# Routing of batches 1 to 7 in one run of products, with the last 64 tokens as 64 by 64 tiles

## The chip, the cores and the metric

The kernel runs on one core of a Trainium2 chip. The metric is the device time of one execution in microseconds (us), as the median of several runs. The core's engines work side by side, each from its own queue in program order: TensorE (PE for its matmuls, PEld for its weight loads), VectorE (DVE), ScalarE (ACT), GpSimd (POOL), and SyncE (SP), which issues transfers.

## The reference, cut to what matters

For 8 batches of 8 heads, 576 tokens and 64 columns, two attentions follow one another: 32 packed rows `p` per head attend to `k`, `v`, and then the tokens `q` attend to the packed result.

```
p_packed = sm_attn(p, k, v)
out      = sm_attn(q, p_packed, p_packed)
x        = out, as 8 * 576 tokens x 512 columns
xn       = x / (|x| + 1e-6);  en = expert_emb / (|expert_emb| + 1e-6)
logits   = xn @ en.T / tau
expert   = argmax(logits);  gate = the largest of softmax(logits)
y[token] = gate * relu(x @ w1[expert]) @ w2[expert]
```

The routing is the part from `xn` to `gate`: for each token the sum of squares of its 512 columns, and its 8 products with the experts' embeddings.

## The kernel before, in words

Each batch is guessed to go to one expert as a whole, whose `w1` and `w2` are loaded; a loop at the end, which runs zero times here, would repair batches for which that fails. While the feed-forward part of batch b runs (`ffn`, L953), the attention of batch b + 1 (`att_main`, L1119) is issued in small steps between its products: the loop at L1504 to L1517 calls one step per step of `ffn` (two where the attention lags behind). All order is written out by hand, and each engine takes its instructions in the order of the program.

`ffn` of a batch has 16 steps of hidden tiles (L1004, evacuated by ACT L1008 and DVE L1009), 8 steps for the last 64 tokens (L1039), and then four output tiles c = 0 to 3 of eight steps of three products each (L1057). An output tile is stored at step f = 2 of the next one (ACT L1406). In c = 3 the weights `w2` of the next batch are split at odd steps (ACT cast L909, POOL subtraction L910), and as soon as the next batch's `lg` exists, its `w1_rows` (L924) go in: products L934 into both pair-banks, then ACT L946 and DVE L947, which make `G`, the weights of the next hidden tiles. At the next batch's start `quarter_banks` (L316) takes the same pair-banks, sets parts of them by DVE (L319, L320), and `quarter_scores` (L331) writes them between the first and the second hidden tile.

PSUM has eight banks of 512 columns: three single ones in rotation ("pf", the accumulators of `ffn`), two pairs ("pb", tiles named pt), and one spare ("pu").

`route` (L757) works on `x.at` (two groups g of four heads, 128 rows by 576 tokens) and `x.ppx` (128 rows by 136 columns: packed values, then 8 columns of embedding products). A product takes 64 rows (one half) and 128 tokens, and gives 136 columns: 128 whose squares sum to the token's squared length, and 8 logits. `sums` squares the 128 columns on ACT with a running sum (L778, an ACTIVATE and a READ_ACCUMULATOR) and adds the 8 columns up on DVE (L781). For batches 1 to 7 it runs in these turns, each at one step of the loop (`TURNS`, L1080, r a step of `route`, f a flip of the next batch's keys, DVE L291):

```
TURNS = "r", "r", "r", "f", "f", "ff", "r", "r", "r", "r", "r"
```

The first turn issues the products of token tiles 0 and 1 into the two pair-banks, turns 1 and 2 their sums; turns 3 to 5 flip keys; turn 6 issues tiles 2, 3 and 4 into the same pair-banks (tile 4, the last 64 tokens, as tiles of 128 whose first half is not used), and turns 7 to 10 their sums and the rest: two adds (L819, L820), the scaling and the argmax (L822 to L834), and a memset on POOL (L838), after which `x.lg` exists. Turn 0 falls on c = 2, f = 0, turn 6 on c = 2, f = 6, and turn 10 on c = 3, f = 2 (for batch 1 one step earlier). Batch 7 has no next batch; its token counts (`counts`, L846) follow three steps later.

Of the kernel before, what the change touches and what calls it, by code (L numbers as in the profile page):

```python
# [9 lines left out]
F32 = mybir.dt.float32  # L10
# [3 lines left out]
AF = mybir.ActivationFunctionType  # L14
ALU = mybir.AluOpType
AX = mybir.AxisListType

P = 128
HB = 4
NC5 = 5  # L20
# [7 lines left out]
def kernel(  # L28
# [12 lines left out]
    nc = tc.nc  # L41
    B, H, S, D = q.shape
    E, DM, F = w1.shape
    NP = p.shape[2]
    NG = H // HB
# [4 lines left out]
    XW = 2 * D + E  # L50
# [6 lines left out]
    sm = ctx.enter_context(tc.tile_pool(name="sm", bufs=2))  # L57
    ps = ctx.enter_context(tc.tile_pool(name="ps", bufs=3, space=bass.MemoryType.PSUM))
    pb = ctx.enter_context(tc.tile_pool(name="pb", bufs=2, space=bass.MemoryType.PSUM))

    pc = ctx.enter_context(tc.tile_pool(name="pc", bufs=1, space=bass.MemoryType.PSUM))
# [11 lines left out]
    for h in range(HB):  # L73
        nc.vector.memset(pairs[32 * h : 32 * h + 32, h // 2 : h // 2 + 1], 1.0)
        for g in range(NG):
            at = (h ^ g) % 2
# [163 lines left out]
    def rows(c):  # L240
        return P if c < 4 else 64
# [513 lines left out]


    def route(x):  # L757
        lg = sm.tile([P, NC5, E], F32, name="lg", tag="lg")
        ss = sm.tile([P, NC5], F32, name="ss", tag="ss")
        nc.gpsimd.memset(lg[:64, 4:5, :], 0.0)  # L760
        nc.gpsimd.memset(ss[:64, 4:5], 1.0)
        def product(c, g, to):
            n = min(c * P, S - P)
            for half in range(2):
                at = slice(64 * half, 64 * half + 64)
                nc.tensor.matmul(  # L766
                    to[:, half],
                    x.at[at, g, n : n + P],
                    x.ppx[at, g],
                    start=True,  # L770
                    stop=True,
                    tile_position=(64 * half, 0),
                )

        def sums(c, pt, lgs, sss):
            r = slice(P - rows(c), P)
            scr = sb.tile([P, 2, NG, 2 * D], F32, name="scr", tag="scr")
            nc.scalar.activation(  # L778
                scr[r, :, : pt.shape[2]], pt[r, :, :, : 2 * D], AF.Square, accum_out=sss[r]
            )  # L780
            nc.vector.tensor_reduce(  # L781
                lgs[r],
                pt[r, :, :, 2 * D :].rearrange("p h g w -> p w h g"),
                axis=AX.XY,
                op=ALU.add,
            )

        def units():
            pt = pb.tile([P, 1024], F32, name="pt", tag="pb")
            return pt.rearrange("p (h w) -> p h w", h=2)[:, :, : 3 * XW].rearrange(  # L790
                "p h (u w) -> p h u w", u=3
            )

        if x is bat[0]:
            for c in range(NC5):
                pt = units()
                for g in range(NG):
                    product(c, g, pt[:, :, g])
                yield
                sums(c, pt[:, :, :NG], lg[:, c], ss[:, c : c + 1])  # L800
        else:
            lg4 = sm.tile([P, E], F32, name="lg4", tag="lg4", bufs=1)
            ss4 = sm.tile([P, 1], F32, name="ss4", tag="ss4", bufs=1)
            for cs in ((0, 1), (2, 3)):
                pts = [units() for _ in cs]
                for c, pt in zip(cs, pts):
                    for g in range(NG):
                        product(c, g, pt[:, :, g])
                if cs[0]:
                    for g, pt in enumerate(pts):  # L810
                        product(4, g, pt[:, :, NG])
                yield
                for c, pt in zip(cs, pts):
                    sums(c, pt[:, :, :NG], lg[:, c], ss[:, c : c + 1])
                    yield
            sums(4, pts[0][:, :, NG:], lg[:, 4], ss[:, 4:5])
            sums(4, pts[1][:, :, NG:], lg4, ss4)
            yield
            nc.vector.tensor_tensor(out=lg[64:, 4], in0=lg[64:, 4], in1=lg4[64:], op=ALU.add)  # L819
            nc.vector.tensor_tensor(out=ss[64:, 4:5], in0=ss[64:, 4:5], in1=ss4[64:], op=ALU.add)  # L820

        nc.vector.tensor_scalar_mul(lg, lg, itau)  # L822
        mx = sm.tile([P, NC5, 1], F32, name="lmx", tag="lmx")
        nc.vector.tensor_reduce(mx, lg, axis=AX.X, op=ALU.max)
        nc.vector.tensor_tensor(
            out=lg, in0=lg, in1=mx.broadcast_to([P, NC5, E]), op=ALU.subtract
        )
        oh = sm.tile([P, NC5, E], F32, name="oh", tag="oh")
        nc.vector.scalar_tensor_tensor(
            out=oh, in0=lg, scalar=0.0, in1=code.broadcast_to([P, NC5, E]),  # L830
            op0=ALU.is_ge, op1=ALU.mult,
        )
        nc.vector.tensor_reduce(mx, oh, axis=AX.X, op=ALU.max)
        nc.vector.tensor_tensor(  # L834
            out=oh, in0=code.broadcast_to([P, NC5, E]), in1=mx.broadcast_to([P, NC5, E]),
            op=ALU.is_equal,
        )
        nc.gpsimd.memset(oh[:64, 4], 0.0)  # L838
        x.oh = oh
        x.lg, x.ss = lg, ss  # L840
# [236 lines left out]
            drain(after.w1g)  # L1077

    AHEAD = 3
    TURNS = "r", "r", "r", "f", "f", "ff", "r", "r", "r", "r", "r"  # L1080
    STF = 2

    def out_rows(b, c):
# [35 lines left out]
    def att_main(b):  # L1119
# [27 lines left out]
        if b:  # L1147
            steps = {"r": route(x), "f": flips}
            if b == 1:
                next(flips)  # L1150
            for turn in TURNS:
                for step in turn:
                    next(steps[step], None)
                yield
# [295 lines left out]
    def route_first():  # L1450
        yield from route(bat[0])
        yield from idle(2)
        counts(bat[0])

    with tc.manual_schedule():
# [65 lines left out]
        out=rest_f, in0=rest_f, scalar1=-1.0, scalar2=float(S), op0=ALU.mult, op1=ALU.add  # L1521
# [6 lines left out]
    with tc.If(n_rest > 0):  # L1528
        with tc.For_i(0, B, 1) as b:
            nb = nc.values_load(rest_i[0:1, ds(b, 1)], min_val=0, max_val=S)  # L1530
            with tc.If(nb > 0):
                x = Batch()
# [3 lines left out]
                drain(att1(x, nat))  # L1536
                drain(att2(x))
                drain(route(x))
                counts(x)
                drain(gates(x))  # L1540
# [5 lines left out]
                    out=ge, in0=x.oh, in1=x.gate.unsqueeze(2).broadcast_to([P, NC5, E]),  # L1546
                    op=ALU.mult,
# [70 lines left out]
```

## Time and profile before

| | us |
|---|---|
| median of 3 runs | 420.41 |
| lowest and highest | 420.27, 420.61 |
| the profiled execution's own time | 420.91 |
| its span, first to last instruction | 419.2 |
| mean granted TensorE clock, share of full speed | 0.995 |

The profile shows one execution. Its own time is the span and what lies around it. Times in the rows below are in us from the span's start, and L12 is line 12 of the kernel. A row of a timeline merges neighbouring instructions of the same kind: start, length, engine, line, operation, what it writes and reads, shapes, count, and in brackets the idle time of the engine before it and what ended it ("issue": nothing that the profile shows).

### The profile page before, as it was taken

The numbers are of one execution on the slowest core, as the hardware profiler recorded it, in microseconds if no ns is written. First come the engines' busy times: TensorE is split into PE (matmuls) and PEld (weight loads), VectorE is DVE, ScalarE is ACT, GpSimd is POOL, SyncE is SP. The second block draws the span as 40 slices with busy tenths as digits, with TensorE's granted clock in tenths as the row PEclk, the third lists the DMA queues.
The fourth block names the chain that finished last, engine by engine and source line by source line (L and its number), as shares of the span: only waits on it lengthen the run. The fifth ranks groups of instructions, "written<-read, shape, count | busy, mean of one in ns | idle before, by whom it ended". The sixth has DMA issues, their size and how long they took to land.

```text
span 419.2 us, 11033 instructions
## 1 busy us (share of the span) xinstructions
PE 408.4 (97%) x4036; PEld 327.9 (78%) x4037; DVE 307.2 (73%) x941; ACT 202.5 (48%) x473; POOL 158.7 (38%) x197
## 2 busy tenths in 40 slices
PE   7899999999999999999999999999999999999993
PEld 4758677697878978698777978789786987779783
DVE  3677696588977889769886889778897798566500
ACT  4577705762365714754146622656146631576110
POOL 2345714437204561336414381136613273142200
PEclk9999999999999999999999999999999999999998
DMA  8999896977999479886999669886899819310012
GB/s 225 331 338 236 220 296 221 229 189 187 298 298 235 116 216 294 284 201 172 267 316 228 169 172 280 301 216 177 225 317 262 195 39 344 121 48 5 20 48 54
DMA packets 42607, 87.93 MB, mean 210 GB/s; under 512 B 11690, under 2 KB 20906, under 8 KB 42546
## 3 DMA queue, kind: packets, MB, share of 16 engines
q1 hardware_dynamic: 35280, 61.44, 54.2%
q0 software_dynamic: 6720, 25.17, 18.4%
q8 instruction: 34, 0.56, 0.6%
q10 hardware_dynamic: 546, 0.54, 0.6%
q14 instruction: 27, 0.22, 0.2%
HBM read 77.68 MB, written 9.44 MB: 208 GB/s over the span
## 4 chain that ended last, share of the span: by engine, by line
PE 91%; DMA 4%; ACT 1%; DVE 1%; POOL 1%; SPq 0%; issue 0%; ACTq 0%; POOLq 0%
PE pf L1057 43%; PE pf L1004 24%; PE pf L1039 7%; PE pt L766 5%; DMA nat<-in_k 4%; PE pt L934 3%; PE pt L396 2%; PE pt L270 2%; PE pt L331 2%; PE pt L1233 1%; PE pu L501 0%; DMA out<-o 0%; PE pt L477 0%; PE pu L512 0%; ACT st L689 0%; PE pt L464 0%
## 5 line engine op out<-in xcount | busy, mean ns | idle before, releaser
L1057 PE MATMUL pf<-w2s,hT 128*128 128x512 f32 (+1 forms) x792 | 183.9, 388 | 0.0
L1057 PEld LDWEIGHTS pf<-w2s,hT 128*128 128x128 f32 x792 | 143.1, 188 | 39.3 <-issue 9.4
L910 POOL TENSOR_TENSOR w2s<-w2r,w2s 128x512 fp32r<-128x512 f32 x64 | 81.2, 1285 | 86.1 <-ACT w2s L909 85.3
L1004 PE MATMUL pf<-AT,G 128*128 128x288 f32 x720 | 102.1, 298 | 0.4 <-DVE hT L1009 0.2
L1004 PEld LDWEIGHTS pf<-AT,G 128*128 128x128 f32 x720 | 97.2, 188 | 4.3 <-issue 1.5
L1009 DVE SCALAR_TENSOR_TENSOR hT<-pf,hT 128x224 fp32r<-128x224 f32 (+1 forms) x128 | 52.2, 413 | 30.3 <-ACT hT L1008 29.9
L1008 ACT ACTIVATE hT<-pf 128x224 fp32r<-128x224 f32 (+1 forms) x128 | 49.3, 386 | 42.8 <-PE pf L1004 40.1
L1406 ACT ACTIVATE o<-pf,gate 128x512 f32<-128x512 f32 (+1 forms) x41 | 26.0, 635 | 32.2 <-PE pf L1057 21.2
L909 ACT CAST w2s<-w2r 128x512 fp32r<-128x512 f32 x64 | 38.7, 618 | 0.2
L291 DVE STREAM_TRANSPOSE kt<-nat 128x576 f32<-128x576 f32 x52 | 38.1, 759 | 0.0
L778 ACT ACTIVATE scr<-pt 128x512 f32<-128x512 f32 (+2 forms) x47 | 25.0, 532 | 18.0 <-PE pt L766 17.0
L1039 PE MATMUL pf<-w2r,h 128*64 128x256 f32 x256 | 33.3, 388 | 0.0
L715 POOL TENSOR_TENSOR AT<-at,AT 128x576 fp32r<-128x576 f32 x7 | 9.9, 1411 | 49.1 <-ACT AT L710 49.1
L383 POOL TENSOR_TENSOR qs<-p 128x320 f32<-128x320 f32 x12 | 10.6, 881 | 45.4 <-ACT p L364 45.4
L689 ACT ACTIVATE st<-st 128x576 f32<-128x576 f32 (+1 forms) x17 | 11.1, 657 | 33.8 <-DVE st L686 32.6
L872 ACT ACTIVATE lg<-lg 128x40 f32<-128x40 f32 x8 | 1.9, 237 | 48.4 <-DVE lg L868 48.4
L781 DVE TENSOR_REDUCE lg<-pt 128x8 f32<-128x32 f32 (+2 forms) x47 | 8.7, 185 | 22.0 <-ACT scr L778 21.7
L766 PEld LDWEIGHTS pt<-ppx,at 64*128 64x128 f32 x320 | 19.7, 186 | 6.2 <-issue 3.6
L1039 PEld LDWEIGHTS pf<-w2r,h 128*64 128x64 f32 x256 | 19.4, 137 | 4.9 <-PE pu L501 1.0
L766 PE MATMUL pt<-ppx,at 64*128 64x136 f32 x320 | 23.1, 287 | 0.0
L710 ACT CAST AT<-at 128x576 fp32r<-128x576 f32 x15 | 10.1, 675 | 22.6 <-DVE at L704 22.5
L364 ACT ACTIVATE p<-pt,qnm 128x160 f32<-128x160 f32 x48 | 17.8, 398 | 0.0
(213 smaller groups left out, 474.9 us busy)
## 6 DMA issues: line engine op xcount, KB each, us to landing
nat<-in_q SPq DMA_DIRECT2D x112, 140.0 KB, 3.5
nat<-in_k SPq DMA_DIRECT2D x96, 140.0 KB, 4.0
w1t<-in_moe_w POOLq DMA_DIRECT2D x12, 1024.0 KB, 9.3
w2r<-in_moe_w POOLq DMA_DIRECT2D x24, 512.0 KB, 16.0
out<-o SPq DMA_DIRECT2D x124, 64.0 KB, 2.1
w2r<-in_moe_w SPq DMA_DIRECT2D x8, 512.0 KB, 10.3
vn<-in_v SPq DMA_DIRECT2D x24, 160.0 KB, 3.8
vn<-in_v SPq DMA_DIRECT2D x48, 80.0 KB, 3.9
```

The costliest lines, as they stand in the source:

```text
L291: nc.vector.transpose(kt.rearrange("p (c i) -> p c i", i=32), t)
L364: nc.scalar.activation(x.p1[g][:, n * QW : n * QW + QW], area(x, g)[:, n // 2, n % 2], AF.Exp, bias=x.nm[:, at : at + 1],)
L766: nc.tensor.matmul(to[:, half], x.at[at, g, n : n + P], x.ppx[at, g], start=True, stop=True, tile_position=(64 * half, 0),)
L778: nc.scalar.activation(scr[r, :, : pt.shape[2]], pt[r, :, :, : 2 * D], AF.Square, accum_out=sss[r])
L909: nc.scalar.copy(t[:, 0], raw)
L910: nc.gpsimd.tensor_tensor(out=t[:, 1], in0=raw, in1=t[:, 0].bitcast(F32), op=ALU.subtract)
L1004: nc.tensor.matmul(pf[:, :HS], w, r, start=(n == 0), stop=(n == len(ops) - 1))
L1008: nc.scalar.activation(hT[:, 0, f, cs], pf[:, :n], AF.Relu)
L1009: nc.vector.scalar_tensor_tensor(out=hT[:, 1, f, cs], in0=pf[:, :n], scalar=0.0, in1=hT[:, 0, f, cs].bitcast(F32), op0=ALU.max, op1=ALU.su ...
L1039: nc.tensor.matmul(pf[64 * hf : 64 * hf + 64, :256], h4[:, f], x.w2r[f // 2][:, f % 2, hf * 256 : hf * 256 + 256], start=(f == 0), stop=(f ...
L1057: nc.tensor.matmul(pf[:, :w], hT[:, a, f, c * P : (c + 1) * P], x.w2s[f][:, m, at : at + w], start=(f == 0 and i == 0), stop=(f == NF - 1 ...
L1406: nc.scalar.activation(o[:, :w], pf[:, :w], AF.Copy, scale=x.gate[:, c : c + 1])
```

## The change

Batches 1 to 7 now issue all routing products in one turn. Token tiles 0 and 1 go to the first two places of the two pair-banks, tile 2 to their third places, tile 3 to the spare bank and one accumulator bank (one row half each), and the last 64 tokens to the third places of these two, as products of 64 rows by 64 token columns at four places of the array (row half by g). `lg` and `ss` become parts of one tile, so that one add can join both. Sums are taken in eight parts, and four small DVE steps join them. The key flips come before the products. Batch 0 keeps its way.

```diff
     def route(x):
-        lg = sm.tile([P, NC5, E], F32, name="lg", tag="lg")
-        ss = sm.tile([P, NC5], F32, name="ss", tag="ss")
+        both = sm.tile([P, NC5, E + 1], F32, name="lg", tag="lg")
+        lg, ss = both[:, :, :E], both[:, :, E]
...
+        def product(at, g, half, to, tokens, column=0):
+            nc.tensor.matmul(
+                to,
+                x.at[at, g, tokens],
+                x.ppx[at, g],
+                start=True,
+                stop=True,
+                tile_position=(64 * half, column),
+            )
...
-            lg4 = sm.tile([P, E], F32, name="lg4", tag="lg4", bufs=1)
-            ss4 = sm.tile([P, 1], F32, name="ss4", tag="ss4", bufs=1)
-            for cs in ((0, 1), (2, 3)):
-                pts = [units() for _ in cs]
-                for c, pt in zip(cs, pts):
-                    for g in range(NG):
-                        product(c, g, pt[:, :, g])
-                if cs[0]:
-                    for g, pt in enumerate(pts):
-                        product(4, g, pt[:, :, NG])
-                yield
-                for c, pt in zip(cs, pts):
-                    sums(c, pt[:, :, :NG], lg[:, c], ss[:, c : c + 1])
-                    yield
-            sums(4, pts[0][:, :, NG:], lg[:, 4], ss[:, 4:5])
-            sums(4, pts[1][:, :, NG:], lg4, ss4)
-            yield
-            nc.vector.tensor_tensor(out=lg[64:, 4], in0=lg[64:, 4], in1=lg4[64:], op=ALU.add)
-            nc.vector.tensor_tensor(out=ss[64:, 4:5], in0=ss[64:, 4:5], in1=ss4[64:], op=ALU.add)
+            pts = [units() for _ in range(2)]
+            ones_of = [
+                pool.tile([P, 512], F32, name=name, tag=name)[:, : 3 * XW].rearrange(
+                    "p (u w) -> p u w", u=3
+                )
+                for pool, name in ((pc, "pu"), (ps, "pf"))
+            ]
+            banks = [[pts[0][:, h], pts[1][:, h], ones_of[h]] for h in range(2)]
+            for c, spots in enumerate((
+                ((0, 0), (0, 1)), ((1, 0), (1, 1)), ((0, 2), (1, 2)), ((2, 0), (2, 1)),
+            )):
+                for g, (n, u) in enumerate(spots):
+                    for half, at in enumerate(halves):
+                        product(at, g, half, banks[half][n][:, u], slice(c * P, c * P + P))
+            for g in range(NG):
+                for half, at in enumerate(halves):
+                    product(
+                        at, g, half, ones_of[half][halves[g], 2], slice(4 * P, S), 64 * g
+                    )
+            yield
+            part = sm.tile([P, 6, E + 1], F32, name="part", tag="pbd", bufs=1)
+            lgx, ssx, every = part[:, :, :E], part[:, :, E], slice(0, P)
+            for n in range(2):
+                sums(every, pts[n][:, :, :NG], lg[:, n], ss[:, n : n + 1])
+                sums(every, pts[n][:, :, NG:], lgx[:, n], ssx[:, n : n + 1])
+                yield
+            for lo, us in ((2, slice(0, NG)), (4, slice(NG, 3))):
+                for n, t in enumerate(ones_of):
+                    sums(every, t[:, us].unsqueeze(1), lgx[:, lo + n], ssx[:, lo + n : lo + n + 1])
+                yield
+            pair = part.rearrange("p (c n) e -> p c n e", n=2)
+            nc.vector.tensor_tensor(
+                out=both[:, 2:4], in0=pair[:, :2, 0], in1=pair[:, :2, 1], op=ALU.add
+            )
+            one, two = part[:, 4], part[:, 5]
+            nc.vector.tensor_tensor(out=one, in0=one, in1=two, op=ALU.add)
+            nc.vector.tensor_copy(two[rest], one[:64])
+            nc.vector.tensor_tensor(out=both[rest, 4], in0=one[rest], in1=two[rest], op=ALU.add)
...
-    TURNS = "r", "r", "r", "f", "f", "ff", "r", "r", "r", "r", "r"
+    TURNS = "", "", "", "f", "ff", "f", "r", "r", "r", "r", "rr"
```

The products thus fall in turn 6, the sums in turns 7 to 10, and `x.lg` exists after turn 10 as before.

## Rows read from the trace of the kernel before

**Rows 1.** The page: busy time of each engine; the chain that ended last.
```profile
PE 408.4 (97%) x4036; PEld 327.9 (78%) x4037; DVE 307.2 (73%) x941; ACT 202.5 (48%) x473; POOL 158.7 (38%) x197
...
PE 91%; DMA 4%; ACT 1%; DVE 1%; POOL 1%; SPq 0%; issue 0%; ACTq 0%; POOLq 0%
```

**Rows 2.** Timeline of TensorE's weight loads, batch 2's routing inside batch 1's outputs.
```profile
113.54 0.87 PEld L1057 LDWEIGHTS pf<-w2s,hT 128*128 128x128 f32 x4
114.76 1.00 PEld L766 LDWEIGHTS pt<-ppx,at 64*128 64x128 f32 x16 [0.35 <-issue]
115.88 3.99 PEld L1057 LDWEIGHTS pf<-w2s,hT 128*128 128x128 f32 x18
120.23 1.46 PEld L766 LDWEIGHTS pt<-ppx,at 64*128 64x128 f32 x24 [0.35 <-DVE kt L291]
121.82 2.59 PEld L1057 LDWEIGHTS pf<-w2s,hT 128*128 128x128 f32 x12
...
129.95 0.95 PEld L1004 LDWEIGHTS pf<-AT,G 128*128 128x128 f32 x6
131.06 0.94 PEld L331 LDWEIGHTS pt<-kt,pw 64*32 64x32 f32 x64 [0.16 <-issue]
```

**Rows 3.** Timeline of ScalarE, the same stretch.
```profile
121.77 0.60 ACT L778 ACTIVATE scr<-pt 128x512 f32<-128x512 f32 x1 [2.30 <-PE pt L766]
...
122.49 0.60 ACT L778 ACTIVATE scr<-pt 128x512 f32<-128x512 f32 x1
...
123.21 0.38 ACT L778 ACTIVATE scr<-pt 64x256 f32<-64x256 f32 x1
...
123.83 0.38 ACT L778 ACTIVATE scr<-pt 64x256 f32<-64x256 f32 x1
...
124.33 0.62 ACT L909 CAST w2s<-w2r 128x512 fp32r<-128x512 f32 x1
```

**Rows 4.** Timeline of VectorE, the same stretch.
```profile
118.29 0.18 DVE L781 TENSOR_REDUCE lg<-pt 128x8 f32<-128x32 f32 x1
...
119.10 2.76 DVE L291 STREAM_TRANSPOSE kt<-nat 128x576 f32<-128x576 f32 x4
...
124.34 0.18 DVE L781 TENSOR_REDUCE lg<-pt 64x8 f32<-64x16 f32 x1 [0.33 <-ACT scr L778]
...
125.33 1.03 DVE L825 TENSOR_TENSOR lg<-lg,lmx 128x40 f32<-128x40 f32 x1
...
126.86 0.20 DVE L834 TENSOR_TENSOR oh<-code,lmx 128x40 f32<-128x40 f32 x1
127.11 2.36 DVE L947 TENSOR_TENSOR G<-pt,G 128x1024 fp32r<-128x1024 f32 x2
...
129.75 0.11 DVE L320 MEMSET pt<- 64x64 f32 x1
```

**Rows 5.** Timeline of GpSimd, the same stretch.
```profile
125.03 1.28 POOL L910 TENSOR_TENSOR w2s<-w2r,w2s 128x512 fp32r<-128x512 f32 x1 [9.51 <-ACT w2s L909]
127.12 0.10 POOL L838 MEMSET oh<- 64x8 f32 x1 [0.82 <-DVE oh L834]
```

**Rows 6.** Timeline of all engines, batch 1's routing.
```profile
75.46 0.24 DVE L822 TENSOR_SCALAR lg<-lg,itau 128x40 f32<-128x40 f32 x1
...
75.97 0.20 DVE L825 TENSOR_TENSOR lg<-lg,lmx 128x40 f32<-128x40 f32 x1
...
76.67 0.20 DVE L834 TENSOR_TENSOR oh<-code,lmx 128x40 f32<-128x40 f32 x1
...
80.59 0.11 DVE L320 MEMSET pt<- 64x64 f32 x1
...
82.39 0.94 PEld L331 LDWEIGHTS pt<-kt,pw 64*32 64x32 f32 x64 [0.16 <-issue]
```

**Rows 7.** Timeline of TensorE's weight loads, batch 7's routing.
```profile
363.68 1.46 PEld L766 LDWEIGHTS pt<-ppx,at 64*128 64x128 f32 x24 [0.35 <-issue]
...
372.36 0.09 PEld L846 LDWEIGHTS pu<-oh,ones 128*1 128x1 f32 x2 [0.35 <-issue]
```

More of the change, by code (lines that the diff above doesn't have):

```diff
@@ L757, in route, with sums @@
     def route(x):
-        lg = sm.tile([P, NC5, E], F32, name="lg", tag="lg")
-        ss = sm.tile([P, NC5], F32, name="ss", tag="ss")
+        both = sm.tile([P, NC5, E + 1], F32, name="lg", tag="lg")
+        lg, ss = both[:, :, :E], both[:, :, E]
         nc.gpsimd.memset(lg[:64, 4:5, :], 0.0)
         nc.gpsimd.memset(ss[:64, 4:5], 1.0)
[L762 to L776, printed above, removed]
+        def product(at, g, half, to, tokens, column=0):
[7 more added lines that the diff above has]
+            )
+        def sums(r, pt, lgs, sss):
             scr = sb.tile([P, 2, NG, 2 * D], F32, name="scr", tag="scr")
+            to = scr.rearrange("p h g w -> p (h g w)")[r, : pt.shape[1] * pt.shape[2] * 2 * D]
             nc.scalar.activation(
-                scr[r, :, : pt.shape[2]], pt[r, :, :, : 2 * D], AF.Square, accum_out=sss[r]
+                to.rearrange("p (h g w) -> p h g w", h=pt.shape[1], g=pt.shape[2]),
+                pt[r, :, :, : 2 * D], AF.Square, accum_out=sss[r],
             )
@@ L792, in units @@
             )
+        rest = slice(64, P)
+        halves = [slice(64 * half, 64 * half + 64) for half in range(2)]
         if x is bat[0]:
@@ L796, in route @@
                 pt = units()
+                n = min(c * P, S - P)
                 for g in range(NG):
-                    product(c, g, pt[:, :, g])
+                    for half, at in enumerate(halves):
+                        product(at, g, half, pt[:, half, g], slice(n, n + P))
                 yield
-                sums(c, pt[:, :, :NG], lg[:, c], ss[:, c : c + 1])
+                sums(slice(P - rows(c), P), pt[:, :, :NG], lg[:, c], ss[:, c : c + 1])
         else:
-            lg4 = sm.tile([P, E], F32, name="lg4", tag="lg4", bufs=1)
@@ L803, in route @@
-            ss4 = sm.tile([P, 1], F32, name="ss4", tag="ss4", bufs=1)
-            for cs in ((0, 1), (2, 3)):
-                pts = [units() for _ in cs]
-                for c, pt in zip(cs, pts):
-                    for g in range(NG):
-                        product(c, g, pt[:, :, g])
-                if cs[0]:
-                    for g, pt in enumerate(pts):
-                        product(4, g, pt[:, :, NG])
-                yield
-                for c, pt in zip(cs, pts):
-                    sums(c, pt[:, :, :NG], lg[:, c], ss[:, c : c + 1])
-                    yield
@@ new lines, in route @@
+            banks = [[pts[0][:, h], pts[1][:, h], ones_of[h]] for h in range(2)]
[6 more added lines that the diff above has]
+            for g in range(NG):
+                for half, at in enumerate(halves):
+                    product(
+                        at, g, half, ones_of[half][halves[g], 2], slice(4 * P, S), 64 * g
+                    )
```

## The prediction

> **What bounds the kernel now.** I read the page first: its engine line and the chain of waits [rows 1]. TensorE is busy 97% of the span and the chain that ended last is 91% TensorE, so time is won or lost only where TensorE's own queue gets shorter or has to wait. [...] The routing products (L766) stand in two groups between the output products (L1057). From the last output load's end to the next output load's start the first group costs 115.88 - (113.54 + 0.87) = 1.47 us with 16 records, the second 121.82 - (115.88 + 3.99) = 1.95 us with 24. The eight records more are two pairs (two row halves side by side, two passes each), so a pair is 0.24 us, and each group has a fixed 1.47 - 4 x 0.24 = 0.51 us, of which 0.35 us is the idle time ahead of it. No stall lies in there: the 0.35 us put down to L291 in the second group is as long as that of the first group, which waits for nothing. So two groups cost 3.42 us a batch, 1.02 us of it for going in and out twice.
>
> Last I followed who must be ready behind the routing: ScalarE's Squares [rows 3], VectorE [rows 4] and GpSimd [rows 5]. Squares, reduces, the argmax steps (L822 to L834), G's low part (L947) and the bank memsets (L319, L320) make one chain that ends in the scores of the next batch (L331, 131.06). The needed memset is done at 129.75 + 0.11 = 129.86, so the chain has 1.2 us of slack and TensorE waits for none of it. The batches repeat: batches 2 to 6 have the same offsets.
>
> **The change, part by part.** *TensorE.* One group instead of two: one fixed 0.51 us goes. Sixteen of the products (eight pairs) stay as they are, 1.92 us. The last 64 tokens were two pairs, 0.48 us; as four tiles of 64 by 64 they go side by side, for which I take one pair's 0.24 us (0.48 would mean that nothing is gained). New is a change of tile shape inside the group, from 64*128 to 64*64. No row shows that one. It can cost nothing, or as much as the idle time on the way in, 0.35; I take the way out, 0.51 - 0.35 = 0.16, because it also follows a short product. New group: 0.51 + 1.92 + 0.24 + 0.16 = 2.83 us, 0.59 less a batch (0.40 to 0.75 by the ends).
> The Trainium skill (TensorEngine Tiling (Array Packing), Key Properties) says that changing the tiling mode, though not the tile, drains the engine, which speaks against the inner change. By that rule it costs as an entry does and the gain is 0.40; the rows cannot tell, having no such change behind short products but the way out.
>
> *Banks.* Besides the two pair-banks the group now takes the spare bank and one of the three accumulator banks. The next use of that accumulator is the second hidden tile of the next batch, some 12 us later, and the spare bank's is later still: cost nothing, covered by c = 3's 24 output products; without that cover a hidden tile would wait for the last Squares.
>
> *ScalarE.* Let T be the first routing load of the new group. It comes when the second group did, less the first group's 1.47: T = 120.23 - 1.47 + 0.04 (the gap between loads that stays) = 118.80. The six Squares, two of which used to be done by then, become eight, all behind T. The first Square of the second group started 1.54 after that group's first load [rows 2, 3], behind the fifth pair, which is the last to write its tile; the new group also has five pairs up to there, so 1.54 stands. A 512-column Square lasts 0.72 until the next, a 256-column one 0.50 to 0.62 (123.83 to 124.33, 123.21 to 123.83); I take 0.50, and by the same slope 0.39 for 128 columns. A reduce never starts before the Square on its banks has ended [rows 3, 4], so I take the reverse too: the Squares on the third unit of a pair-bank wait for the reduce ahead of them, 0.27 us each, twice (lower end: no wait). The Trainium skill (PSUM — Partial Sum Buffer, on bank collisions) has two engines kept apart on a bank for reads as well. That gives T + 1.54, 2.52, 3.02, 3.97, 4.47, 4.97; then the w2 cast (L909, issued after turn 9, so now between the Squares) from 5.47 with 0.62; the last two Squares at 6.09 and 6.48; the last reduce at 6.90. In the old order the last reduce came at 124.34 - 120.23 = 4.11 behind its group.
>
> *VectorE.* The four key flips (2.76 us) move ahead of all reduces. They can start at 118.29, where the first group's first reduce stands now, and end at 121.05, just when the first reduce wants to start (T + 2.26): no cost. The sums now take four small steps in place of two. The first is a two-input add from SBUF, as L825 is: that one takes 1.03 us while GpSimd's L910 runs and ends 0.05 behind it [rows 4, 5], but 0.20 in batch 1, where no L910 runs beside it [rows 6]. GpSimd's L910 starts 0.70 behind the start of the cast: 5.47 + 0.70 + 1.28 = 7.45, so the add ends at 7.50 (without the lock 7.3). Copy and second add at 0.24 each (five steps take 1.21 in [rows 6]): L822 at 7.98. From there to the end of L834 it is 1.41 unlocked [rows 6]: L825 now gains 0.83, because the next L910 stands behind the memset L838 in GpSimd's queue, and that waits for L834. L834 ends at 9.40, L947 starts at 9.45, the first pair of memsets ends 2.75 later as it does now [rows 4], and L331 can start 0.05 after: T + 12.25, that is 131.05.
>
> *What waits for it.* TensorE without a stall would come to the hidden tile at 129.95 - 0.59 = 129.36 and to L331 1.11 later. The first half of G is ready at T + 9.45 + 1.18 (half of the 2.36 in [rows 4]) = 129.43, a wait of 0.07; then L331, at 130.54, waits for the memsets until 131.05. Before, it started at 131.06. So in batches 2 to 6 the stall takes back the 0.59: gain 0.0.
>
> *Batches 1 and 7.* In batch 1 the memset is done at 80.70 and L331 starts at 82.39, a slack of 1.7 [rows 6]; the cast stands behind all Squares there and no L910 runs beside the adds, so the chain shifts by less and 0.59 stays. In batch 7 there are no memsets, but the count (L846, at 372.36 [rows 7]) wants L838, which comes at T + 9.6 with T = 363.68 - 1.43 = 362.25, so 371.9 with its end, against 371.77: 0.45 stays.
>
> *Other queues.* The flips' freed buffers let SP issue the query loads under a microsecond earlier; the kernel waits for no load there, cost nothing. GpSimd's two memsets of the sums move from turn 0 to turn 6, into idle time.
>
> **Sum.** 0.59 + 5 x 0.0 + 0.45 = 1.0 us less. The profiled execution took 420.91 (span 419.2 and 1.7 around it), so it would take 419.9; the median of the runs is 0.5 lower, 420.41, and so is the forecast: 419.4.
>
> **Rivals.**
> *The gain stays everywhere.* If the Squares on the third units need not wait for the reduces, the chain is 0.54 shorter, L331 could start at 130.51 and TensorE would be there at 130.47. For it: no row shows a Square behind a reduce. Against: the reduces wait for the Squares every time. Gain 6 x 0.59 + 0.45 = 4.0, time 416.4. With the drain of the Trainium skill (TensorEngine Tiling (Array Packing), Key Properties) it would be 6 x 0.40 + 0.26 = 2.7, time 417.7.
> *The chain is longer and the kernel slower.* Place: L331's wait for the memsets in batches 2 to 6. If the four 256-column Squares take 0.62 instead of 0.50, L331 comes 0.48 later than now, 5 x 0.48 - 1.0 = 1.4 us slower, 421.8. For it: one of the two Squares of that size does take 0.62. Against: the other doesn't. It decides from a delay of 0.38 a batch on; a further wait of the same size anywhere between the first Square and L947 does the same.
> *The quad gains nothing.* The four tiles run as two pairs: batches 1 and 7 lose 0.24 each, the others are set by the chain all the same; 0.5 us less in all, 419.9, no change that could be told.
>
> **How the numbers follow.** About 0.2%, 0.84 us, is what a measurement of this kernel can tell from no change. The forecast (stall takes back the gain, L331 within 0.3 us of its old place) has 0.57: -1.0 - 5 x 0.3 to -1.0 + 5 x 0.3, 417.9 to 420.9; it falls in two, about 0.31 faster and 0.26 within 0.2%. The whole gain has 0.18, the longer chain 0.20, the quad without gain 0.05. Faster 0.31 + 0.18 = 0.49, same 0.26 + 0.05 = 0.31, slower 0.20. The range, 417.0 to 421.9, leaves out the lower half of the whole gain and what lies above a delay of 0.5.
>
> **What would show it.** In the changed profile L766 stands once per batch with 0.35 idle ahead of it and 40 records in about 2.3 us from first load to last. The second Square starts behind the first reduce, not directly behind the first Square. L825 takes 0.2 in all batches, and L331 has idle time of about 0.6 us ahead of it, ended by VectorE's memsets, in batches 2 to 6 but not in batch 1. It is wrong if L331 waits for nothing (the gain is then 3 us or more), if idle time shows up at L1057 or L1004 outside these places, or if a hidden tile waits for an accumulator bank.

## The result and the profile after

The changed kernel takes 423.27 us, the median of 14 runs, against 420.99 for the kernel before in as many: 1.0054 of it, 95% interval 1.0039 to 1.0069. It is slower by 2.3 us, where 1.0 us less was forecast and the range ended at 421.9. Both kernels scatter by some 2.5 us from execution to execution, part of it in the first 35 us, ahead of any routing; what follows therefore compares stretches inside the profiles.

The page of the changed kernel: the engines' busy time, and the chain that ended last, by engine and by line.

```profile
PE 407.5 (96%) x4036; PEld 326.6 (77%) x4037; DVE 308.3 (73%) x969; ACT 202.9 (48%) x501; POOL 158.6 (38%) x197
...
PE 67%; DVE 12%; DMA 9%; ACT 6%; issue 3%; SPq 1%; POOL 1%; ACTq 0%; DVEq 0%; POOLq 0%
PE pf L1080 26%; PE pf L1027 23%; PE pf L1062 6%; DMA nat<-in_k 6%; ACT scr L776 4%; DVE G L970 3%; DMA out<-o 3%; PE pt L764 2%; PE pt L396 2%; PE pt L331 2%; PE pt L270 1%; PE pt L957 1%; DVE kt L291 1%; DVE lg L837 1%; SPq L194 1%
```

TensorE is busy 0.9 us less than in [rows 1], yet its share of the chain fell from 91% to 67%: followed back from its end, the chain now leaves TensorE for the routing's Squares (L776) and VectorE's steps. That share says which path was followed, not how long TensorE stands still: of the kernels below, "early store" has 68% and is faster than the kernel before, and "order alone" has 91% with a gap of 2.42 us. Where TensorE waits, and for how long, the weight loads tell. Here are those of batch 1's routing in the changed kernel (L764 is the routing product, L1080 the output product, L957 `w1_rows`).

```profile
70.08 1.46 PEld L764 LDWEIGHTS pt<-ppx,at 64*128 64x128 f32 x24 [0.35 <-DVE pw L299]
72.53 1.23 PEld L1080 LDWEIGHTS pf<-w2s,hT 128*128 128x128 f32 x6 [0.18 <-issue]
76.62 1.23 PEld L1080 LDWEIGHTS pf<-w2s,hT 128*128 128x128 f32 x6 [2.87 <-issue]
78.27 0.23 PEld L957 LDWEIGHTS pt<-w1t,T 64*32 64x32 f32 x16 [0.42 <-issue]
79.13 0.22 PEld L957 LDWEIGHTS pt<-w1t,T 64*32 64x32 f32 x8 [0.63 <-issue]
79.98 0.22 PEld L957 LDWEIGHTS pt<-w1t,T 64*32 64x32 f32 x8 [0.64 <-issue]
81.70 3.97 PEld L1080 LDWEIGHTS pf<-w2s,hT 128*128 128x128 f32 x18 [1.51 <-issue]
...
86.83 0.94 PEld L331 LDWEIGHTS pt<-kt,pw 64*32 64x32 f32 x64 [0.16 <-issue]
```

Six output products behind the routing, that is two steps, TensorE stands still for 2.87 us. These are the last two steps of c = 2; what waits is the first product of c = 3. Batches 2 to 7 have no such gap: their longest idle time between weight loads is 0.84 us, as in the kernel before. The chain of waits names what ended it (start, length, what):

```profile
76.11 0.20 ACT scr L776
76.31 0.02 issue
76.34 0.17 DVE part L780
76.51 0.09 DVE lg L837
76.60 0.05 issue
76.65 1.69 PE pf L1080 x6
```

The routing's last Square, its last reduce on the accumulator bank (L780, done at 76.51), then the output tile. L837, the first add, stands in between only because it runs on the same engine: TensorE's queue begins to take its next work at 76.55, just behind the reduce and before L837 ends at 76.59. ScalarE's stores (L1429) on both sides of the gap show why that bank was needed: c = 0 is stored ahead of the routing's Squares, c = 1 only in c = 3, behind the gap.

```profile
69.88 0.68 ACT L1429 ACTIVATE o<-pf,gate 128x512 f32<-128x512 f32 x1
...
78.16 0.68 ACT L1429 ACTIVATE o<-pf,gate 128x512 f32<-128x512 f32 x1
```

The loads behind the gap are also slower: the 32 records of L957 and what lies around them take 81.70 - 78.27 = 3.43 us. The windows view shows why (PE, PEld, DVE, ACT and POOL busy, granted clock, DMA share, GB/s):

```profile
76.62:78.27 1.65, 1.62 (x6) 1.05 (x6) 1.34 (x8) 0.64 (x2) 0.00 (x0) 0.94 0.91 240
78.27:81.70 3.43, 3.43 (x33) 0.66 (x32) 0.65 (x3) 1.94 (x3) 1.37 (x2) 0.53 1.11 242
81.70:85.70 4.00, 4.00 (x25) 3.30 (x18) 2.58 (x6) 2.86 (x5) 3.42 (x3) 1.00 1.07 239
```

In the stretch that begins 1.65 us behind the gap the granted clock is 0.53, nearly all of it at 1.2 GHz instead of 2.4, and is back at 1.00 in the stretch from 81.70.

Batch 2 went much as predicted, some 4.4 us later in the span. Its weight loads, where [rows 2] show the kernel before:

```profile
123.30 1.46 PEld L764 LDWEIGHTS pt<-ppx,at 64*128 64x128 f32 x24 [0.35 <-issue]
...
125.75 2.61 PEld L1080 LDWEIGHTS pf<-w2s,hT 128*128 128x128 f32 x12 [0.18 <-issue]
...
133.90 0.95 PEld L1027 LDWEIGHTS pf<-AT,G 128*128 128x128 f32 x6
135.40 0.96 PEld L331 LDWEIGHTS pt<-kt,pw 64*32 64x32 f32 x64 [0.55 <-PE pf L1027]
```

Its Squares, in place of [rows 3]:

```profile
124.84 0.60 ACT L776 ACTIVATE scr<-pt 128x512 f32<-128x512 f32 x1 [2.20 <-PE pt L764]
...
125.78 0.39 ACT L776 ACTIVATE scr<-pt 128x256 f32<-128x256 f32 x1 [0.26 <-DVE lg L780]
...
126.29 0.60 ACT L776 ACTIVATE scr<-pt 128x512 f32<-128x512 f32 x1
...
127.24 0.39 ACT L776 ACTIVATE scr<-pt 128x256 f32<-128x256 f32 x1 [0.26 <-DVE lg L780]
...
128.63 0.61 ACT L932 CAST w2s<-w2r 128x512 fp32r<-128x512 f32 x1
```

And VectorE, in place of [rows 4]:

```profile
125.56 0.19 DVE L780 TENSOR_REDUCE lg<-pt 128x8 f32<-128x32 f32 x1
...
129.94 0.17 DVE L780 TENSOR_REDUCE part<-pf 128x8 f32<-128x8 f32 x1 [0.23 <-ACT scr L776]
130.02 0.61 DVE L837 TENSOR_TENSOR lg<-part 128x18 f32<-128x18 f32 x1
...
131.73 0.20 DVE L848 TENSOR_TENSOR lg<-lg,lmx 128x40 f32<-128x40 f32 x1
...
132.54 2.35 DVE L970 TENSOR_TENSOR G<-pt,G 128x1024 fp32r<-128x1024 f32 x2
...
135.17 0.11 DVE L320 MEMSET pt<- 64x64 f32 x1
```

The second and fourth Squares wait 0.26 us each for a reduce; the first add (L837) takes 0.61 and ends 0.03 behind GpSimd's subtraction (L933, from 129.32 to 130.60); the argmax subtraction (L848, 1.03 us in [rows 4]) takes 0.20; and L331 has 0.55 us of idle time ahead of it, 0.16 before. The view of that line names what ended the idle time in batches 2 to 6 (sum in us, times), first that ahead of its weight loads, then that ahead of its products:

```profile
  PE pf L1027: 2.7, 5
  DVE pt L320: 1.7, 5
```

The products wait for the memset L320, and so does the first load, though its row names the hidden tile: it starts at 135.40, behind the memset's end at 135.17 + 0.11 = 135.28, while the hidden tile's last load ends at 133.90 + 0.95 = 134.85. The memset thus holds TensorE five times.

All profiles of this study, cut into the same stretches by the weight loads (us; "first hidden tile" is the start of the first one in batch 0 with `G` as weights, "batch 1" is from there to L331 of batch 2, "batches 2 to 6" from there to L331 of batch 7, "batch 7" from there to its first hidden tile; "time" is the median of all runs, and the ratio to the kernel before and its 95% interval come from the same sets of runs, though the ratio is not the quotient of the two medians):

| kernel | first hidden tile | batch 1 | batches 2 to 6 | batch 7 | time | ratio | interval |
|---|---|---|---|---|---|---|---|
| before | 34.63 | 47.76 | 243.44 | 47.96 | 420.99 | | |
| changed | 35.15 | 51.68 | 242.89 | 47.48 | 423.27 | 1.0054 | 1.0039 to 1.0069 |
| changed, again | 35.21 | 49.99 | 242.93 | 47.48 | 423.11 | 1.0040 | 1.0022 to 1.0057 |
| early store | 34.54 | 47.30 | 242.88 | 47.45 | 419.22 | 0.9952 | 0.9933 to 0.9972 |
| batch 1 old | 34.55 | 47.84 | 242.94 | 47.45 | 419.80 | 0.9969 | 0.9953 to 0.9985 |
| early store and order | 34.26 | 47.22 | 240.94 | 47.46 | 417.74 | 0.9922 | 0.9903 to 0.9942 |
| order alone | 36.26 | 49.61 | 240.97 | 47.46 | 420.97 | 0.9986 | 0.9972 to 1.0000 |
| before, early store | 34.78 | 47.85 | 243.61 | 47.99 | 421.20 | 1.0004 | 0.9990 to 1.0017 |

The changed kernel loses 3.9 us in batch 1, gains 0.11 in each of the next five, and 0.5 in batch 7. The start differs by up to 2.0 us between profiles, before any routing.

### The profile page after: what moved, and what is told of

Same layout as the page of the kernel before. It is cut to its first block, busy times and chain, and to the rows that moved or that the text cites. A ratio compares the mean times of both kernels' runs of the same rounds, so it can differ in the third digit from the quotient of the medians.

```text
span 423.0 us, 11100 instructions
## 1 busy us (share of the span) xinstructions
PE 407.5 (96%) x4036; PEld 326.6 (77%) x4037; DVE 308.3 (73%) x969; ACT 202.9 (48%) x501; POOL 158.6 (38%) x197
## 4 chain that ended last, share of the span: by engine, by line
PE 67%; DVE 12%; DMA 9%; ACT 6%; issue 3%; SPq 1%; POOL 1%; ACTq 0%; DVEq 0%; POOLq 0%
PE pf L1080 26%; PE pf L1027 23%; PE pf L1062 6%; DMA nat<-in_k 6%; ACT scr L776 4%; DVE G L970 3%; DMA out<-o 3%; PE pt L764 2%; PE pt L396 2%; PE pt L331 2%; PE pt L270 1%; PE pt L957 1%; DVE kt L291 1%; DVE lg L837 1%; SPq L194 1%
## 5 line engine op out<-in xcount | busy, mean ns | idle before, releaser
L1080 PE MATMUL pf<-w2s,hT 128*128 128x512 f32 (+1 forms) x792 | 182.1, 387 | 2.5 <-DVE lg L837 2.5
L1080 PEld LDWEIGHTS pf<-w2s,hT 128*128 128x128 f32 x792 | 143.6, 188 | 42.5 <-issue 14.3
L933 POOL TENSOR_TENSOR w2s<-w2r,w2s 128x512 fp32r<-128x512 f32 x64 | 80.9, 1283 | 85.0 <-ACT w2s L932 82.7
L1429 ACT ACTIVATE o<-pf,gate 128x512 f32<-128x512 f32 (+1 forms) x41 | 26.0, 634 | 27.3 <-PE pf L1080 16.4
L776 ACT ACTIVATE scr<-pt 128x512 f32<-128x512 f32 (+2 forms) x33 | 16.8, 508 | 20.3 <-PE pt L764 16.4
L970 DVE TENSOR_TENSOR G<-pt,G 128x1024 fp32r<-128x1024 f32 x14 | 16.5, 1217 | 3.1 <-ACT G L969 3.1
L922 POOL DMA_DIRECT2D w2r<-in_moe_w x24 | 17.0, 713 | 0.0
L764 PEld LDWEIGHTS pt<-ppx,at 64*128 64x128 f32 x208 | 12.7, 187 | 3.7 <-issue 2.5
```

The source lines that it names most:

```text
L764: nc.tensor.matmul(to, x.at[at, g, tokens], x.ppx[at, g], start=True, stop=True, tile_position=(64 * half, column),)
L776: nc.scalar.activation(to.rearrange("p (h g w) -> p h g w", h=pt.shape[1], g=pt.shape[2]), pt[r, :, :, : 2 * D], AF.Square, accum_out=sss[r],)
L933: nc.gpsimd.tensor_tensor(out=t[:, 1], in0=raw, in1=t[:, 0].bitcast(F32), op=ALU.subtract)
L970: nc.vector.tensor_tensor(out=to[1], in0=src, in1=to[0].bitcast(F32), op=ALU.subtract)
L1080: nc.tensor.matmul(pf[:, :w], hT[:, a, f, c * P : (c + 1) * P], x.w2s[f][:, m, at : at + w], start=(f == 0 and i == 0), stop=(f == NF - 1 ...
L1429: nc.scalar.activation(o[:, :w], pf[:, :w], AF.Copy, scale=x.gate[:, c : c + 1])
```

## The experiments

The theory: the output tile c = 3 of batch 0 waits for the accumulator bank that the routing has borrowed, because the tiles of c = 1 and c = 2 still hold the other two. The rivals put the loss on an accident of one execution, on every batch instead of batch 1, or on the longer chain by itself; the expectations give each its numbers. The kernel before was run again beside them: 421.22 us beside the first four, 420.98 beside the last two.

**The changed kernel again**, unaltered.

> The changed kernel once more, unaltered. Both theories expect the same +2.3 us against the kernel before (0.5%). What it tells: whether batch 1's idle time of 2.9 us ahead of the last output tile of batch 0 (c = 3) and the low granted clock behind it (0.53 of full speed from 78.3 to 81.7 us in the first profile) come again. Theory A (accumulator bank): the idle time comes again at the same place, within 0.3 us, since it hangs on the order of the program alone. Theory B (a late transfer or another disturbance of that one execution): it moves or goes.

Measured: 1.0040, interval 1.0022 to 1.0057. The gap came again, to the hundredth, but the low clock did not; the weight loads, then the windows view:

```profile
76.59 1.23 PEld L1080 LDWEIGHTS pf<-w2s,hT 128*128 128x128 f32 x6 [2.87 <-issue]
78.18 0.18 PEld L957 LDWEIGHTS pt<-w1t,T 64*32 64x32 f32 x16 [0.36 <-issue]
```

```profile
76.59:78.18 1.59, 1.56 (x7) 1.05 (x7) 1.28 (x8) 0.59 (x2) 0.00 (x0) 1.00 0.98 239
78.18:80.05 1.87, 1.87 (x33) 0.48 (x32) 0.38 (x2) 1.29 (x3) 1.38 (x2) 1.00 1.09 223
```

L957's stretch takes 1.87 us here and 3.43 in the first profile. So the gap belongs to the program's order and is no accident of one execution (theory B falls), and the clock is a second price, which the first profile paid and this one did not. Of the 24 executions of the two sets, 12 have a mean granted clock of 0.992 or less, and their median is 423.8; the other 12 have 0.994 or more, and 422.4. Among 26 executions of the three kernels below without the gap there is none under 0.995, and of 48 of the kernel before, run beside these and the later experiments, two are at 0.992. A mean does not tell where the clock was low, though: the profile of "order alone" below has 0.993, with 0.84 and 0.82 from 5 to 15 us, ahead of any routing, and 1.00 behind its gap. That the gap brings the lower clock is thus suggested, and not shown.

**Early store.** `ffn` of batch 0 keeps its output tiles one longer (`late`); the edit lets c = 1 be stored in c = 2, and with it c = 2 in c = 3 instead of at the end.

```diff
-                    if f == STF and len(last) > late:
+                    while f == STF and len(last) > (late and c < 2):
                         store(*last.pop(0))
```

> One edit: the feed-forward part of batch 0 stores its output tile c = 1 two steps into c = 2, together with c = 0, instead of two steps into c = 3. Theory A: batch 0 stores one tile late, so at the start of c = 3 the accumulators of c = 1 and c = 2 are still held and the only bank left is the one that the routing took; c = 3 waits for the routing's last Square and reduce. With c = 1 stored early its bank is free: no idle time ahead of c = 3, no low clock, batch 1 gains 0.5 us instead of losing 3.9. Whole kernel 1.6 us less than the kernel before (0.5 in batch 1, 0.12 in each of batches 2 to 6, 0.5 in batch 7). Theory B (the long chain of Squares, reduces and adds itself holds TensorE, whatever bank c = 3 takes): the idle time stays at 2.5 us or more and the time stays 2.3 us above the kernel before.

Measured: 0.9952 (0.9933 to 0.9972), about 2.0 us less than the kernel before. ScalarE's two stores ahead of the Squares, then the weight loads of batch 1:

```profile
69.26 1.26 ACT L1429 ACTIVATE o<-pf,gate 128x512 f32<-128x512 f32 x2
```

```profile
69.45 1.46 PEld L764 LDWEIGHTS pt<-ppx,at 64*128 64x128 f32 x24 [0.35 <-DVE pw L299]
71.90 2.61 PEld L1080 LDWEIGHTS pf<-w2s,hT 128*128 128x128 f32 x12 [0.18 <-issue]
74.87 0.18 PEld L957 LDWEIGHTS pt<-w1t,T 64*32 64x32 f32 x16 [0.35 <-issue]
```

All twelve output loads run through and the gap is gone, while the Squares, the reduces and TensorE's order are unchanged. The store of c = 2 cannot have done it, since it comes only within c = 3. So it was the bank, not the chain by itself. Batch 1 takes 47.30 us, 0.46 less than before; the other stretches stay as in the changed kernel.

**Batch 1 the old way**: the old branch of `route` and the old turns for batch 1 alone.

```diff
+        elif x is bat[1]:
+            for cs in ((0, 1), (2, 3)):
...
-            for turn in TURNS:
+            for turn in FIRST if b == 1 else TURNS:
...
+    FIRST = "r", "r", "r", "f", "f", "ff", "r", "r", "r", "r", "r"
```

> Batch 1 alone is routed the old way (two groups of products, old turns); batches 2 to 7 stay as changed. Theory A: the whole loss sits in batch 1, so the time is 1.1 us less than that of the kernel before (5 x 0.12 + 0.5), with no stretch of low clock. Rival C (the loss is spread: the accumulator or the longer chain costs in every batch): the time stays above the kernel before, by 1 us or more.

Measured: 0.9969 (0.9953 to 0.9985), 1.3 us less. Batch 1 is back at 47.84 us (47.76 before), the rest as changed: the whole loss sat in batch 1, and rival C falls.

**Early store and another order of the Squares.**

```diff
             for n in range(2):
                 sums(every, pts[n][:, :, :NG], lg[:, n], ss[:, n : n + 1])
-                sums(every, pts[n][:, :, NG:], lgx[:, n], ssx[:, n : n + 1])
-                yield
+            yield
+            for n in range(2):
+                sums(every, pts[n][:, :, NG:], lgx[:, n], ssx[:, n : n + 1])
+            yield
```

> The early store of the run before, and the Squares in another order: first the two of 512 columns on the two pair-banks, then the two of 256 columns on their third places, so that none follows the reduce of its own banks directly. Theory A (the prediction's chain: in batches 2 to 6 the scores of the next batch wait for the memsets, and two Squares wait 0.26 us each for a reduce): the chain is 0.5 us shorter, the idle time of 0.55 us ahead of the next batch's scores shrinks to the 0.16 us of the kernel before, and each of batches 2 to 6 gains 0.4 to 0.5 us: 3.6 to 4.1 us less than the kernel before. Rival D (that idle time comes from something else than this chain): the same 1.6 us less as with the early store alone, and the 0.55 us stay.

Measured: 0.9922 (0.9903 to 0.9942), 3.3 us less by the ratio and 3.5 by the medians, a little short of the 3.6 to 4.1 expected. ScalarE, then the weight loads, of batch 2:

```profile
119.48 0.60 ACT L776 ACTIVATE scr<-pt 128x512 f32<-128x512 f32 x1 [2.18 <-PE pt L764]
...
120.20 0.60 ACT L776 ACTIVATE scr<-pt 128x512 f32<-128x512 f32 x1
...
120.92 0.38 ACT L776 ACTIVATE scr<-pt 128x256 f32<-128x256 f32 x1
```

```profile
128.54 0.95 PEld L1029 LDWEIGHTS pf<-AT,G 128*128 128x128 f32 x6
129.66 0.94 PEld L331 LDWEIGHTS pt<-kt,pw 64*32 64x32 f32 x64 [0.16 <-issue]
```

No Square waits for a reduce, L331 has its old 0.16 us, and batches 2 to 6 take 240.94, that is 0.50 us a batch less than before and 0.39 less than with the early store alone. The chain from the Squares to the memsets was what took their gain back; rival D falls. This version beats both kernels.

**The order alone**, with the stores as late as in the changed kernel (the last edit without the one before).

> The other order of the Squares alone, with the stores of batch 0 as late as in the changed kernel. Theory A: batch 1's idle time ends with the last reduce of the routing, which comes 0.5 us sooner, so 2.87 becomes 2.35 us; batches 2 to 6 gain 0.5 each as with the early store. Against the kernel before: batch 1 loses 2.35 - 0.59, about 1.8, the others gain 3.0, so 1.2 us less if the clock stays up, up to 0.4 more if the low clock follows the idle time as it did in the first profile of the changed kernel (1.6 us). Rival (the idle time is set by a transfer or by the store, not by the reduce): it stays at 2.87.

Measured: 0.9986 (0.9972 to 1.0000), 0.6 us less by the ratio and none by the medians (420.97 against 420.98), where 1.2 less to 0.4 more was expected; its profile lost 1.6 us in the start. The weight loads of batch 1:

```profile
73.61 1.23 PEld L1082 LDWEIGHTS pf<-w2s,hT 128*128 128x128 f32 x6 [0.19 <-issue]
77.26 1.23 PEld L1082 LDWEIGHTS pf<-w2s,hT 128*128 128x128 f32 x6 [2.42 <-issue]
```

With a chain shorter by about half a microsecond the gap shrinks from 2.87 to 2.42 (2.35 expected): its end is the last reduce. Batch 1 costs 1.85 us more than before, and batches 2 to 6 gain 0.49 each, as with the early store and the new order together.

**The kernel before with the early store**: the edit of the store made there.

> A control: the kernel before with the early store of batch 0 alone. Theory A: nothing to gain, since there c = 3 takes the bank of c = 0, which is stored in time: within 0.3 us of the kernel before, no gap moved. Rival (storing earlier is worth something by itself, whatever the routing does): about as much less as the early store brought to the changed kernel.

Measured: 1.0004 (0.9990 to 1.0017), no difference. The early store brings nothing by itself that these runs can tell; it takes away what the change had brought in.

## Why the prediction was wrong

**The step that failed** is *Banks*: "The next use of that accumulator is the second hidden tile of the next batch, some 12 us later ...: cost nothing". That holds for batches 2 to 7, where no output or hidden tile waits longer than before. It was read from batch 2 [rows 2 to 4] and carried over to batch 1, whose routing runs in batch 0's `ffn`; there `late` holds each output tile back by one more: that an output tile is stored at step f = 2 of the next one, as the part on the kernel before has it, is not so in batch 0. When c = 3 begins, c = 1 and c = 2 are both unstored, the routing has the third bank, and c = 3 waits for the routing's last reduce. The step named its cover ("c = 3's 24 output products") and what comes without it, a wait for the last Squares, but looked for that wait at a hidden tile of every batch, not at an output tile of one. The early store shows it, and the control shows that storing earlier is worth nothing where no bank is borrowed. The prediction had named idle time at the output products (L1057, now L1080) as a sign that it is wrong; that is where it came.

**Its size.** Batch 1 was to gain 0.59 us. In the profile without the low clock it loses 49.99 - 47.76 = 2.2 us, the gap less what the routing saves; in the other 3.9. The prediction had no term for the clock.

**What held.** *TensorE's terms*, in batch 2: from the last output load before the group (0.35 us ahead of 123.30) to the next at 125.75 it is 2.80 us against 2.83. The change of tile shape inside was taken at 0.16 us; in the trace the last 64*128 load ends at 125.03 + 0.19 = 125.22 and the first 64*64 one starts at 125.35, 0.13 us of idle time:

```profile
125.03 0.19 PEld L764 LDWEIGHTS pf<-ppx,at 64*128 64x128 f32 x1
...
125.35 0.13 PEld L764 LDWEIGHTS pu<-ppx,at 64*64 64x64 f32 x1
```

The Trainium skill (TensorEngine Tiling (Array Packing), Key Properties) has a change of mode drain the engine, and this trace agrees: idle time stands at the change. It is 0.13 us here, between two shapes behind a short product, and not the 0.35 of the entry from full tiles behind a 512-column one; whether the shapes or the product's length make the difference, no run separates.

*ScalarE and VectorE*: from T = 123.30 the first Square came at 1.54 (1.54 forecast), the second at 2.48 (2.52), the fourth at 3.94 (3.97), the cast at 5.33 (5.47), the last reduce at 6.64 (6.90), L970, which is L947 of before, at 9.24 (9.45), L331 at 12.10 (12.25). The two waits for a reduce, the first add held beside GpSimd and the quick L848 are all there. Two sums of the working are off and did no harm. By its own terms the fourth Square is due at 3.02 + 0.72 + 0.27 = 4.01, not 3.97. And three small steps follow the locked add, not two: the add ended at 7.33 (7.50 forecast) and L845, which is L822 of before, started at 7.92 (7.98), 0.59 later where 0.48 was allowed. That this came out is luck, the earlier end of the add making up for the step left out.

*The stall at L331*: the prediction had batches 2 to 6 gain 0.0 each; they gained 0.11: the chain was 0.15 shorter than worked out, and the group began 0.06 later in the batch. The reordered Squares show that this chain, with the two waits in it, took back another 0.4. Batch 7 gained 0.48 against 0.45.

**The rivals.** The whole gain, 4.0 us, is what the early store and the new order together come near, with 3.3 to 3.5. The longer chain gave the right sign for the wrong reason: its place was L331, where the chain proved shorter. The quad ran as one: its eight loads start within 0.1 us of each other.

## What to carry to other kernels

A buffer borrowed from a rotating pool is returned when its last reader has run, and the price is paid by whoever next finds the pool empty: list for each stage where the borrowing happens how many buffers are held at that point, and do it separately for the first and the last round, where a special case (here a store one tile later) may hold one more. When a chain on other engines has 1 us of slack behind a bound engine, joining its work into one burst uses it up; ordering the burst so that neighbours do not share a bank won back 0.4 us a batch.

## What the runs showed of the hardware

The same gap of 2.87 us in TensorE's weight loads was followed by a granted clock of 1.00 in one profile ("changed, again") and in another ("changed") by 3.4 us at 0.53, a difference of 1.6 us in that stretch; behind the 2.42 us of "order alone" it stayed at 1.00. The Trainium skill (TensorE: Matmul & The Clock Gate, Part 1) has the half rate follow idle time; of these three profiles one agrees.

Squares and reduces on disjoint columns of one bank ran one after the other in both directions: the reduce behind the Square, as in [rows 3, 4], and the next Square behind the reduce, 0.26 us each time. In the trace each waits for a semaphore that the other sets, so this is the order that the program keeps; what the chip would do without it no run shows.
